# Attention row factors spread by a selection product instead of a round trip through DRAM, in a gated mix of attention and a gated feed-forward layer

## The chip, the cores and the metric

The kernel runs on one core of one Trainium2 chip. Time is device time in microseconds (us). Three runs of the kernel before gave a median of 1131.39 us (1130.17 to 1133.29). Engines are named as in the profile: PE (TensorE matmul), PEld (its weight loads), DVE (VectorE), ACT (ScalarE), POOL (GpSimd), SP (SyncE). A name with a q behind it (ACTq, SPq) is that engine's sequencer while it issues a DMA.

## The reference, cut to what matters

One input x of 2048 rows and 640 columns goes through a causal attention with a compressive memory (32 heads of width 20, four segments of 512 rows), through a gated feed-forward layer (hidden width 1728), and the two are mixed by a gate of each row.

```python
for s in range(N):                              # 4 segments of L = 512 rows
    logits = einsum("bhqd,bhkd->bhqk", qs, ks) * scale + mask
    p = softmax(logits)
    a_dot = einsum("bhqk,bhkd->bhqd", p, vs)
    num = einsum("bhld,bhde->bhle", phi(qs), M)
    den = einsum("bhld,bhd->bhl", phi(qs), z)[..., None] + 1e-6
    outs.append(g * num / den + (1.0 - g) * a_dot)   # g = sigmoid(beta), one per head
    M = M + einsum("bhld,bhle->bhde", phi(ks), vs)
    z = z + einsum("bhld->bhd", phi(ks))
a = stack(outs) @ wo
b = (silu(x @ w1) * (x @ w3)) @ w2
out = gate * a + (1 - gate) * b                 # gate = sigmoid((x * gate_w).sum(-1))
```

## The kernel before, in words

**Layout.** Everything is kept turned: features on partitions, the 512 rows of a segment c along the free axis. A matrix of 640 features is five blocks of 128 partitions. Single-precision products are done in three passes (high by high, high by low, low by high), so that one 128x512 output of a projection is a group of 15 matmuls in one PSUM bank. PSUM's eight banks are handed out in a ring (`bank_tile`, L110): a product that is spread over several steps holds its bank until it is filled, all others take the next in order, and a bank is taken again when its last reader is done.

**Order of the work.** The order on PE is the program's, written by hand. Attention runs as a fixed sequence of visits (`attention`, L744): for each group of four heads a long visit (score products `s`, transposed score products `t`, and the products `o` with the values) and a short one. Between visits a driver (the loop at L940) steps through a list of dense jobs (projections `q`, `k`, `v`, the feed-forward's `g`, `u` up and `f` down, the output projection `op`) in generators: each `yield` gives the time in ns that the step counts for. A yield that is a whole number also counts as a step for loading and splitting weights (`w_step`, L172), for late stores, and for `braid` (L839), which puts one step of a second generator behind every so many whole steps of a first. A yield that is a float (699.0) is no such step. `after(n, f)` (L727) runs f a number of slots later. The orders on DVE, ACT, POOL and SP are chosen by a scheduler at build time, except where `here(...)` pins an instruction to its program order. On each engine instructions run in order, and a DMA issue that waits holds up what is behind it.

**Around the change.** `pv_quad` (L626) writes each four heads' unscaled outputs and their row sums to DRAM (`od`). When the last heads of a segment are done, `o_sums` (L646) loads the sums as a 128x128 tile `rs` (32 heads by 4 pieces on partitions) and the gate's factors as `er`; 16 slots later `o_scale` (L667) takes the reciprocal on DVE (L669) and multiplies by (1-g) and the gate (L670). Then four DMAs issued by ACT (L672) write each head's factors 20 times to DRAM (`rd`, 32x20x512), and five more issued by ACT (`load_factor`, L682, issue at L686) read it back as five 128x512 tiles `rb`, through a ring of two buffers named `spread`, which the gate's own tile `sh` (`load_share`, L688) shares.

`normalize` (L703) is the first half of the output projection's job: for each of the five blocks DVE multiplies `oall` by `rb` (L711); from segment 1 on PE turns the memory's part with four transposes (`gt`, L715) and DVE adds it (L716); ACT rounds to the high part (L717) and DVE takes the low part (L718). It is braided into other work: for segment 0 and 2 into two up projections, one step behind every 3; for segment 1 into up projections, every 3 after 11; for segment 3, in the tail, into a down projection and up projections, every 3 after 10.

`ffn_down` (L516) fills one bank for each block of 128 outputs. With three hidden blocks that is 9 matmuls, with the last group (one whole and one half block) 5. The first 3 matmuls are a step that yields 699.0. For segment 0 the last down projection is braided with `split_x` (L237) of segments 2 and 3: ACT rounds x, copies it to a PSUM bank (`xh`) and DVE takes the difference (`X`, L131); what is left of segment 3's five blocks when the braid's first job ends is issued in a row.

Of the kernel before, what the change touches and what calls it, by code (L numbers as in the profile page):

```python
# [38 lines left out]
def gated_mix(ctx: ExitStack, tc: tile.TileContext, xT, wqk, wv, w13, w2, w2h, wo, beta, out):  # L39
# [9 lines left out]
    od = [dp.tile([H, 32, L], F32, name=f"od{c}") for c in range(NSEG)]  # L49
    gd = [dp.tile([P, 4, D], F32, name=f"gd{c}") for c in range(NSEG)]  # L50
    ed = [dp.tile([2, 4, P], F32, name=f"ed{c}") for c in range(NSEG)]
    rd = [dp.tile([H, DH, L], F32, name=f"rd{c}") for c in range(NSEG)]


    ident = cp.tile([P, P], F32, name="ident")
# [2 lines left out]
    vg = [cp.tile([P, 4, VG + 12], F32, name=f"vg{i}") for i in range(NVG)]  # L58
    gH = cp.tile([P, H], F32, name="gH")
    cR = cp.tile([P, 1], F32, name="cR")  # L60
    rs = cp.tile([P, P], F32, name="rs")
    er = cp.tile([P, P], F32, name="er")
    et = cp.tile([8, P], F32, name="et")
    nsT = [cp.tile([P, 32], FR, name=f"ns{i}") for i in range(2)]
    gate = cp.tile([P, NSEG, 2, 4], F32, name="gate")
    Ms = {}
# [13 lines left out]
    def gates():  # L80
        here(nc.sync.dma_start(gH, beta.rearrange("(o h) -> o h", o=1).broadcast_to([P, H])))
        for i in range(4):
            here(nc.sync.dma_start(cR[i::4], beta.rearrange("(h o) -> h o", o=1)))
        for g in (gH, cR):
            here(nc.scalar.activation(g, g, AF.Exp, scale=-1.0))
            here(nc.vector.tensor_scalar(g, g, 1.0, None, op0=ALU.add))

        nc.vector.reciprocal(cR, cR)
        nc.vector.tensor_scalar(cR, cR, -1.0, 1.0, op0=ALU.mult, op1=ALU.add)

    here = tc.keep_in_program_order
    last = {}
# [286 lines left out]

    def gate_turn(c):  # L380
        ps = bank_tile(f"ge{c}")
        nc.tensor.transpose(ps[:8, :P], gate[:, c].rearrange("p x a -> p (x a)"), ident)
        nc.scalar.copy(et, ps[:8, :P])
        store_later(ed[c].rearrange("x a p -> (x a) p"), et, ("e", c))
# [131 lines left out]
    def ffn_down(cs, js, idx, last=()):  # L516
        first = js[0] == 0
        w2s = [w_get(i, idx[0]) for i in idx]
        for c in cs:
            if c in last:  # L520
                load_share(c)
            if first:
                accs[c] = slot(f"acc{c}")[:, :KB * L].rearrange("p (b n) -> p b n", b=KB)
            for fb in range(KB):
                ps = bank_tile(f"f{c}_{js[0]}_{fb}", 1300 if len(js) > 2 else 690)
                ms = []
                for j, w in zip(js, w2s):
                    for a, b in (PASSES if j < NF else ((0, 0), (0, 1))):
                        ms.append((w[:, b, fb * P:(fb + 1) * P], hts[c, j][:, a, :]))
                for n, (w, h) in enumerate(ms):  # L530
                    nc.tensor.matmul(ps, w, h, start=n == 0, stop=n == len(ms) - 1)  # L531
                    if n % 3 == 2 and n < len(ms) - 1:
                        yield 699.0 if n == 2 else 699
                filled()
                dst = accs[c][:, fb]
                if first:
                    nc.scalar.copy(dst, ps)
                elif c not in last:
                    nc.vector.tensor_add(dst, ps, dst)
# [106 lines left out]
    def o_sums(c):  # L646
        assert ("e", c) in stored
        here(nc.sync.dma_start(rs, od[c][:, DH].rearrange("h (a n) -> h a n", n=P)))
        here(nc.sync.dma_start(er, ed[c][1:2].broadcast_to([H, 4, P])))
        after(16 if c < NSEG - 1 else 3, o_scale, c)  # L650
        if c == NSEG - 1:
            o_load(c, KB - 1)
        else:
            after(6, o_load, c, KB - 1)

    def o_load(c, b):

# [6 lines left out]
            else:  # L664
                here(nc.sync.dma_start(dst, od[c][h, e:e + n]))

    def o_scale(c):  # L667

        here(nc.vector.reciprocal(rs, rs))  # L669
        nc.vector.scalar_tensor_tensor(rs, rs, cR, er, op0=ALU.mult, op1=ALU.mult)  # L670
        for a in range(4):
            here(nc.scalar.dma_start(rd[c][:, :, a * P:(a + 1) * P], rs[a::4].unsqueeze(1).broadcast_to([H, DH, P])))  # L672
        turned.append(c)
        for b in range(2):
            after(8 + b, load_factor, c, b)

    shares, factors = {}, {}

    def spread(name):
        return sp.tile([P, L], F32, tag="spread", name=name, bufs=2)  # L680

    def load_factor(c, b):  # L682
        if b < KB and (c, b) not in factors:
            assert c in turned
            factors[c, b] = spread(f"rb{c}_{b}")
            here(nc.scalar.dma_start(factors[c, b], rd[c].rearrange("h e n -> (h e) n")[b * P:(b + 1) * P]))  # L686
# [15 lines left out]

    def normalize(c):  # L703

        load_factor(c, 0)
        load_factor(c, 1)
        if not c:
            gms[c] = big_tile(f"oT{c}", FR)[:, :KB * L].rearrange("p (b n) -> p b n", b=KB)
        for b in range(KB):
            o, hi = factors[c, b], gms[c][:, b]  # L710
            nc.vector.tensor_mul(o, oall[c][:, b].bitcast(F32), o)  # L711
            if c:
                pt = bank_tile(f"gt{c}_{b}")
                for qb in range(4):
                    nc.tensor.transpose(pt[:, qb * P:(qb + 1) * P], hi[:, qb * P:(qb + 1) * P].bitcast(F32), ident)  # L715
                nc.vector.tensor_add(o, o, pt)  # L716
# [10 lines left out]
    def after(n, f, *a):  # L727
        soon.append([n, f, a])
# [147 lines left out]
    d = job_down(A, 2)  # L876
    u = [job_up(A, j) for j in GROUPS[3][:2]]
    o1, o2 = jobs_oproj(0)
    seg = [d, braid(chain(u), o1, 3), o2] + [job_up(A, j) for j in GROUPS[3][2:]] + [job_down(A, 3)]
# [16 lines left out]
    segs.append((2 * H + LAG + 2, seg))  # L896
    up.append(job_up(B, 2))
    o1, o2 = jobs_oproj(1)
    seg = [braid(chain(up[1:]), o1, 3, 11), braid(o2, job_read(3), 3, 1), job_down(B, 0), braid(chain(jobs_up(B, 1)), (0, load_memory(2)), 5)]
# [4 lines left out]
    seg = [d, braid(chain(u), o1, 3), o2] + [job_up(B, j) for j in GROUPS[2][2:]]  # L904
# [120 lines left out]
```

## Time and profile before

| | before |
|---|---|
| median of 3 runs | 1131.39 us (1130.17 to 1133.29) |
| the profiled execution's own time | 1133.55 us |
| its span, first to last instruction | 1131.7 us |
| mean granted TensorE clock | 0.987 |
| PE busy | 1099.8 us (97%), 6265 matmuls |
| DVE / ACT / POOL busy | 588.0 / 460.3 / 491.1 us |

The profile is one execution. In a view in order of time a row gives the start, the length, the engine (or its sequencer, q), the line in the kernel, the operation, output<-input, and in brackets the idle time of that engine before the row and what ended it; rows merge instructions of one kind that follow one another. In a view by stretches each engine has its busy time (and its instructions in brackets), and PEclk is the clock that TensorE was granted, as a share of full speed.

### The profile page before, as it was taken

To read this page: it belongs to the slowest core of one execution; us is meant where nothing else is said; L and a number is where in the kernel's file an instruction comes from. 1 tells how busy PE (TensorE), PEld (TensorE's weight loads), DVE (VectorE), ACT (ScalarE), POOL (GpSimd) and SP (SyncE) were. 2 spreads that over 40 slices of the span, in tenths; PEclk is the share of its full clock that TensorE was granted. 3 is DMA by queue.
4 is the path that set the end of the run, shared out by engine and by line. 5 is a ranking of instruction groups with operands and counts; after the bars stand their busy time and mean duration, and the time that the engine had idled before them with its cause. 6 is when DMAs were issued, how large, how long until landed. Compare 5 with 4: busy or idle time off the path is not lost.

```text
span 1131.7 us, 17920 instructions
## 1 busy us (share of the span) xinstructions
PE 1099.8 (97%) x6265; PEld 855.7 (76%) x6265; DVE 588.0 (52%) x1692; ACT 460.3 (41%) x952; POOL 491.1 (43%) x598
## 2 busy tenths in 40 slices
PE   9999999999999999998999996999999999999998
PEld 6988877777777777786977774776776777777786
DVE  5032564455555545474253674884556675561465
ACT  6255334543243324255365632535534353333130
POOL 4053444455353336233253343554754464354142
PEclk9999999999999999998999997999999899999999
DMA  8265943343455425434385967555656343543423
GB/s 319 87 234 202 267 110 90 93 119 90 100 120 137 121 68 163 125 110 131 112 270 201 296 197 185 133 158 132 168 135 160 98 125 91 119 107 87 121 77 112
DMA packets 99193, 163.29 MB, mean 144 GB/s; under 512 B 10432, under 2 KB 34272, under 8 KB 99104
## 3 DMA queue, kind: packets, MB, share of 16 engines
q1 hardware_dynamic: 61312, 105.91, 29.9%
q0 software_dynamic: 20384, 38.68, 15.4%
q10 hardware_dynamic: 17408, 17.57, 4.9%
q8 instruction: 50, 0.82, 0.3%
q14 instruction: 39, 0.32, 0.1%
HBM read 101.80 MB, written 59.79 MB: 143 GB/s over the span
## 4 chain that ended last, share of the span: by engine, by line
PE 78%; issue 8%; DMA 5%; DVE 4%; POOL 3%; ACT 2%; ACTq 1%; SPq 0%; DVEq 0%; POOLq 0%
PE g L251 15%; PE f L531 15%; PE u L251 14%; PE q L251 6%; PE k L251 6%; PE o L631 5%; PE op L788 4%; PE s L578 4%; PE v L362 3%; PE t L611 3%; PE pm L425 1%; DVE junk L585 1%; POOL W L106 1%; PE nd L329 1%; DMA rb<-rd 1%
## 5 line engine op out<-in xcount | busy, mean ns | idle before, releaser
L106 POOL TENSOR_TENSOR W<-wr,W 128x640 fp32r<-128x640 f32 (+1 forms) x126 | 197.9, 1576 | 287.9 <-ACT W L105 263.1
L585 DVE CUSTOM_DVE_ANT_0 junk<-s,mask 128x256 bf16<-128x256 f32 (+3 forms) x512 | 250.4, 489 | 118.8 <-PE s L578 86.6
L617 ACT ACTIVATE P<-t 128x512 f32<-128x512 f32 (+1 forms) x384 | 172.0, 538 | 146.4 <-PE t L611 116.0
L251 PE MATMUL g<-X,W 128*128 128x512 f32 x840 | 209.8, 398 | 1.5 <-ACT P L617 1.4
L531 PE MATMUL f<-ht,W 128*128 128x512 f32 x820 | 198.4, 400 | 0.0
L251 PE MATMUL u<-X,W 128*128 128x512 f32 x780 | 196.5, 399 | 0.3 <-DVE m L585 0.3
L251 PEld LDWEIGHTS g<-X,W 128*128 128x128 f32 x840 | 155.6, 188 | 38.4 <-ACT P L617 1.6
L531 PEld LDWEIGHTS f<-ht,W 128*128 128x128 f32 x820 | 154.9, 191 | 37.3 <-issue 0.2
L621 POOL TENSOR_SCALAR_AFFINE_SELECT P<-P 128x256 f32<-128x256 f32 x192 | 94.0, 500 | 195.8 <-ACT P L617 195.2
L251 PEld LDWEIGHTS u<-X,W 128*128 128x128 f32 x780 | 143.8, 188 | 35.7 <-DVE m L585 1.2
L105 ACT CAST W<-wr 128x640 fp32r<-128x640 f32 (+1 forms) x133 | 95.7, 728 | 111.6 <-PE f L531 24.8
L106 POOL TENSOR_TENSOR ht<-ft,ht 128x512 fp32r<-128x512 f32 x52 | 68.0, 1307 | 97.3 <-ACT ht L105 97.3
L631 PE MATMUL o<-P,vg 128*32 128x512 f32 (+3 forms) x1024 | 79.8, 455 | 9.9 <-DVE rb L716 9.5
L555 POOL DMA_DIRECT2D qk<-qkd x128 | 82.8, 649 | 3.4 <-PE t L611 2.5
L578 PE MATMUL s<-qk 60*128 60x256 f32 (+3 forms) x512 | 77.4, 348 | 4.2 <-DVE oq L635 2.7
L251 PE MATMUL k<-X,W 128*128 128x512 f32 x300 | 77.0, 403 | 0.9 <-ACT P L617 0.9
L251 PE MATMUL q<-X,W 128*128 128x512 f32 x300 | 73.8, 400 | 1.4 <-ACT X L105 0.6
L631 PEld LDWEIGHTS o<-P,vg 128*32 128x32 f32 x1024 | 31.0, 113 | 54.6 <-issue 44.7
L362 PE MATMUL v<-W,X 128*128 128x320 f32 (+1 forms) x480 | 71.8, 311 | 0.0
L362 PEld LDWEIGHTS v<-W,X 128*128 128x128 f32 x480 | 71.1, 189 | 0.4
L611 PE MATMUL t<-qk 62*128 62x256 f32 (+3 forms) x512 | 65.0, 326 | 6.2 <-DVE X L131 3.6
L251 PEld LDWEIGHTS q<-X,W 128*128 128x128 f32 x300 | 55.6, 189 | 16.6 <-ACT W L105 1.2
(107 smaller groups left out, 1096.0 us busy)
## 6 DMA issues: line engine op xcount, KB each, us to landing
qk<-qkd POOLq DMA_DIRECT2D x128, 240.0 KB, 4.2
wr<-in_w_dram SPq DMA_DIRECT2D x80, 320.0 KB
qkd<-qs SPq DMA_DIRECT2D x20, 512.0 KB
qkd<-ks SPq DMA_DIRECT2D x20, 512.0 KB
od<-oq SPq DMA_DIRECT2D x32, 256.0 KB
wr<-in_wo_dram SPq DMA_DIRECT2D x20, 320.0 KB
vg<-vd SPq DMA_DIRECT2D x16, 336.0 KB
xr<-in_xT_dram SPq DMA_DIRECT2D x20, 256.0 KB
```

The lines of the kernel that those rows point to most:

```text
L105: pin(nc.scalar.copy(dst[:, 0], src))
L106: (lo or nc.gpsimd.tensor_sub)(dst[:, 1], src, dst[:, 0].bitcast(F32))
L251: nc.tensor.matmul(ps, w[:, a, kb * P:(kb + 1) * P], x[:, b, kb, :], start=n == 0, stop=n == 14)
L362: nc.tensor.matmul(ps[:, :n1 - n0], x[:, a, kb, lb * P:(lb + 1) * P], wvt[kb][:, b, n0:n1], start=n == 0, stop=n == 14)
L531: nc.tensor.matmul(ps, w, h, start=n == 0, stop=n == len(ms) - 1)
L555: here(nc.gpsimd.dma_start(t[64 * i:64 * i + RH], qkd[c][RH * (h + i):RH * (h + i + 1)]))
L578: nc.tensor.matmul(ps[i][:, o:o + w], q[:, qb * P:(qb + 1) * P], key[:, :w], start=n == 0, stop=n == len(todo) - 1, skip_group_check=True)
L585: nc.vector.tensor_tensor_reduce(out=junk[:, :w], in0=ps[i][:, o:o + w], in1=mask[:, L - w:], scale=1.0, scalar=-3.0e38, op0=ALU.add, op1= ...
L611: nc.tensor.matmul(ps[i][:, o:o + L - kb * P], key[:, kb * P:(kb + 1) * P], q[:, kb * P:], start=n == 0, stop=n == len(todo) - 1, skip_gro ...
L617: last["exp"] = nc.scalar.activation(pairs[2 * m + k]["P"][:, i, o:o + n], ps[i][:, b:b + n], AF.Exp, scale=SCALE)
L621: nc.gpsimd.affine_select(d, d, pattern=[[0, 2], [0, n], [1, P]], base=0, channel_multiplier=-1, compare_op=ALU.is_ge, fill=0.0)
L631: nc.tensor.matmul(ps[32 * i:32 * i + 32, kb * P:], heads[2 * p + i]["v"][:, kb], pairs[p + i // 2]["P"][:, i % 2, o:o + n], start=kb == 0 ...
```

## The change

1. `rd` in DRAM, its four writes and the five reads of `rb` go. In their place DVE splits the 128x128 factors into three bfloat16 parts (two copies and two differences), and three DMAs issued by SP, pinned in order, lay the parts out as one tile `rR` of 96 partitions by 512 (three times 32 heads).
2. A constant `sel` of 96x640 in bfloat16 is made once on POOL: three times the same 32x640 matrix of ones and zeros that is one where the column belongs to the row's head.
3. `normalize` takes a bank for each block, fills it with one matmul of `sel`'s 128 columns with `rR` (`rr`), and DVE multiplies `oall` by that bank into a tile of the ring `f`. One step of 700 for a block replaces two steps.
4. `o_scale` comes 22 slots after the sums instead of 16. The braids that carry `normalize` take a step behind every 5 (segments 0 and 2) or 4 (segments 1 and 3) instead of 3, and its time in the plan is 3.5 instead of 0 or 2.3.
5. The tile `spread` goes; `sh` has a buffer of its own or, for segment 3, one of the ring `f`. `er` and `et` move to a ring of two that the memory's update uses.
6. In `ffn_down` the first step of a fill of 5 matmuls yields 699 instead of 699.0, so that such a fill counts as two steps.

```diff
-    rd = [dp.tile([H, DH, L], F32, name=f"rd{c}") for c in range(NSEG)]
+    sel = cp.tile([96, D], BF, name="sel")
     rs = cp.tile([P, P], F32, name="rs")
-    er = cp.tile([P, P], F32, name="er")
-    et = cp.tile([8, P], F32, name="et")
+    rp = cp.tile([P, 3, P], BF, name="rp")
+    rR = cp.tile([96, L], BF, name="rR")
...
+    def selection():
+        here(nc.gpsimd.memset(sel, 1.0))
+        nc.gpsimd.affine_select(sel[:32], sel[:32], pattern=[[1, D]], base=0, channel_multiplier=-DH,
+                                compare_op=ALU.is_ge, fill=0.0)
+        nc.gpsimd.affine_select(sel[:32], sel[:32], pattern=[[-1, D]], base=DH - 1, channel_multiplier=DH,
+                                compare_op=ALU.is_ge, fill=0.0)
+        for i in (32, 64):
+            nc.gpsimd.tensor_copy(sel[i:i + 32], sel[:32])
...
     def gate_turn(c):
+        et = sp.tile([8, P], F32, tag="mt", name=f"et{c}", bufs=2)
...
                     if n % 3 == 2 and n < len(ms) - 1:
-                        yield 699.0 if n == 2 else 699
+                        yield 699.0 if n == 2 and len(ms) > 5 else 699
...
     def o_sums(c):
+        er = sp.tile([P, P], F32, tag="mt", name=f"er{c}", bufs=2)
         here(nc.sync.dma_start(er, ed[c][1:2].broadcast_to([H, 4, P])))
-        after(16 if c < NSEG - 1 else 3, o_scale, c)
+        after(22 if c < NSEG - 1 else 3, o_scale, c, er)
...
+    def o_scale(c, er):
+        here(nc.vector.reciprocal(rs, rs))
+        nc.vector.scalar_tensor_tensor(rs, rs, cR, er, op0=ALU.mult, op1=ALU.mult)
+        nc.vector.tensor_copy(rp[:, 0], rs)
+        nc.vector.tensor_sub(rs, rs, rp[:, 0])
+        nc.vector.tensor_copy(rp[:, 1], rs)
+        nc.vector.tensor_sub(rp[:, 2], rs, rp[:, 1])
+        for i in range(3):
+            here(nc.sync.dma_start(rR[32 * i:32 * i + 32].rearrange("h (a n) -> h a n", n=P), rp[:, i]))
+        turned.append(c)
...
-    def o_scale(c):
-        here(nc.vector.reciprocal(rs, rs))
-        nc.vector.scalar_tensor_tensor(rs, rs, cR, er, op0=ALU.mult, op1=ALU.mult)
-        for a in range(4):
-            here(nc.scalar.dma_start(rd[c][:, :, a * P:(a + 1) * P], rs[a::4].unsqueeze(1).broadcast_to([H, DH, P])))
-        turned.append(c)
-        for b in range(2):
-            after(8 + b, load_factor, c, b)
-    def load_factor(c, b):
-        if b < KB and (c, b) not in factors:
-            factors[c, b] = spread(f"rb{c}_{b}")
-            here(nc.scalar.dma_start(factors[c, b], rd[c].rearrange("h e n -> (h e) n")[b * P:(b + 1) * P]))
     def load_share(c):
-        shares[c] = spread(f"sh{c}")
+        shares[c] = f_tile("sh") if c == NSEG - 1 else sp.tile([P, L], F32, tag="share", name=f"sh{c}", bufs=1)
...
     def normalize(c):
-        load_factor(c, 0)
-        load_factor(c, 1)
         for b in range(KB):
-            o, hi = factors[c, b], gms[c][:, b]
-            nc.vector.tensor_mul(o, oall[c][:, b].bitcast(F32), o)
+            o, hi = f_tile(f"on{c}_{b}"), gms[c][:, b]
+            ps = bank_tile(f"rr{c}_{b}")
+            nc.tensor.matmul(ps, sel[:, b * P:(b + 1) * P], rR, start=True, stop=True)
+            nc.vector.tensor_mul(o, oall[c][:, b].bitcast(F32), ps)
...
             nc.vector.tensor_sub(oall[c][:, b], o, hi.bitcast(F32))
-            yield 450 if c else 1
-            load_factor(c, b + 2)
-            yield 1
+            yield 700
...
-        return (2.3 if c else 0, a), (17.5, b)
+        return (3.5, a), (17.5, b)
...
-    seg = [d, braid(chain(u), o1, 3), o2] + ...
+    seg = [d, braid(chain(u), o1, 5), o2] + ...
-    seg = [braid(chain(up[1:]), o1, 3, 11), ...
+    seg = [braid(chain(up[1:]), o1, 4, 11), ...
-    tail = [braid(chain([d] + u), o1, 3, 10)] + [o2, job_down(B, 4, B)]
+    tail = [braid(chain([d] + u), o1, 4, 10)] + [o2, job_down(B, 4, B)]
...
+        elif n == 4:
+            selection()
```

More of the change, by code (lines that the diff above doesn't have):

```diff
@@ L654, in o_sums @@
             after(6, o_load, c, KB - 1)
+    def o_scale(c, er):
[8 more added lines that the diff above has]
+        turned.append(c)
+    shares = {}
     def o_load(c, b):
@@ L665, in o_load @@
                 here(nc.sync.dma_start(dst, od[c][h, e:e + n]))
-    def o_scale(c):
-        here(nc.vector.reciprocal(rs, rs))
-        nc.vector.scalar_tensor_tensor(rs, rs, cR, er, op0=ALU.mult, op1=ALU.mult)
-        for a in range(4):
-            here(nc.scalar.dma_start(rd[c][:, :, a * P:(a + 1) * P], rs[a::4].unsqueeze(1).broadcast_to([H, DH, P])))
-        turned.append(c)
-        for b in range(2):
-            after(8 + b, load_factor, c, b)
-    shares, factors = {}, {}
-    def spread(name):
-        return sp.tile([P, L], F32, tag="spread", name=name, bufs=2)
-    def load_factor(c, b):
-        if b < KB and (c, b) not in factors:
-            assert c in turned
-            factors[c, b] = spread(f"rb{c}_{b}")
-            here(nc.scalar.dma_start(factors[c, b], rd[c].rearrange("h e n -> (h e) n")[b * P:(b + 1) * P]))
     def load_share(c):
-        shares[c] = spread(f"sh{c}")
+        shares[c] = f_tile("sh") if c == NSEG - 1 else sp.tile([P, L], F32, tag="share", name=f"sh{c}", bufs=1)
         here(nc.scalar.dma_start(shares[c], ed[c][0].rearrange("a n -> (a n)").unsqueeze(0).broadcast_to([P, L])))
@@ L703, in normalize @@
     def normalize(c):
-        load_factor(c, 0)
-        load_factor(c, 1)
+        assert c in turned
         if not c:
@@ L878, in gated_mix @@
     o1, o2 = jobs_oproj(0)
-    seg = [d, braid(chain(u), o1, 3), o2] + [job_up(A, j) for j in GROUPS[3][2:]] + [job_down(A, 3)]
+    seg = [d, braid(chain(u), o1, 5), o2] + [job_up(A, j) for j in GROUPS[3][2:]] + [job_down(A, 3)]
     u0, u1 = jobs_up_by_chunk(A, 4)
@@ L898, in gated_mix @@
     o1, o2 = jobs_oproj(1)
-    seg = [braid(chain(up[1:]), o1, 3, 11), braid(o2, job_read(3), 3, 1), job_down(B, 0), braid(chain(jobs_up(B, 1)), (0, load_memory(2)), 5)]
+    seg = [braid(chain(up[1:]), o1, 4, 11), braid(o2, job_read(3), 3, 1), job_down(B, 0), braid(chain(jobs_up(B, 1)), (0, load_memory(2)), 5)]
     segs.append((3 * H + LAG + 1, seg))
@@ L903, in gated_mix @@
     o1, o2 = jobs_oproj(2)
-    seg = [d, braid(chain(u), o1, 3), o2] + [job_up(B, j) for j in GROUPS[2][2:]]
+    seg = [d, braid(chain(u), o1, 5), o2] + [job_up(B, j) for j in GROUPS[2][2:]]
     seg += [job_down(B, 2), braid(chain(jobs_up(B, 3)), (0, load_memory(3)), 5)]
```

## The prediction

> **What bounds the kernel now.** I read the page's busy shares first, then what PE waited for, then PE's busy time in stretches of 20 us, and last the order of time in the stretches that fall short.
>
> ```profile
> span 1131.7 us, 17920 instructions
> PE 1099.8 (97%) x6265; PEld 855.7 (76%) x6265; DVE 588.0 (52%) x1692; ACT 460.3 (41%) x952; POOL 491.1 (43%) x598
> PE o L631 <- DVE rb L716: 9.5, 1, 9.5
> core 0: us, PE busy (x) PEld busy (x) DVE busy (x) ACT busy (x) POOL busy (x), PEclk, DMA share, GB/s
> 383.00:403.00 20.00, 19.49 (x95) 15.05 (x96) 14.41 (x36) 9.67 (x20) 9.78 (x13) 1.00 0.42 120
> 503.00:523.00 20.00, 16.02 (x78) 10.71 (x81) 12.77 (x23) 11.52 (x21) 7.81 (x13) 0.89 0.52 169
> 686.00:706.00 20.00, 10.18 (x63) 5.78 (x63) 6.55 (x12) 4.41 (x8) 3.61 (x4) 0.67 0.58 163
> 869.00:889.00 20.00, 17.26 (x101) 12.20 (x100) 10.20 (x31) 5.42 (x13) 4.21 (x8) 0.83 0.41 113
> 1053.00:1089.00 36.00, 36.00 (x168) 29.33 (x167) 20.58 (x29) 8.70 (x14) 7.92 (x5) 1.00 0.40 122
> ```
>
> PE sets the end: it is idle for 1131.7 - 1099.8 = 31.9 us, and everything else hides behind it. So an edit is worth what it takes from PE's idle time, from the time at a lower granted clock, or adds to PE's stream. Three stretches hold 3.98 + 9.82 + 2.74 = 16.5 us of the idle time, and they alone (the last with its neighbours) show a clock under 1. Segment 0's (383 to 403) loses 0.51 us, segment 3's (1053 to 1089) nothing. The worst of the three is segment 1's normalize:
>
> ```profile
> 684.20 5.85 ACTq L672 DMA_DIRECT2D rd<-rs x4
> 694.75 0.81 ACTq L686 DMA_DIRECT2D rb<-rd x2
> 698.55 1.37 DVE L711 TENSOR_TENSOR rb<-oall,rb 128x512 f32<-128x512 f32 x2 [5.96 <-DMA rb<-rd]
> 700.77 4.49 PE L631 MATMUL o<-P,vg 128*32 128x512 f32 x32 [9.46 <-DVE rb L716]
> 849.07 2.36 PE L631 MATMUL o<-P,vg 128*32 128x512 f32 x32
> 877.07 0.79 PE L578 MATMUL s<-qk 60*128 60x384 f32 x3 [2.74 <-DVE oq L635]
> 877.79 8.55 PE L531 MATMUL f<-ht,W 128*128 128x512 f32 x24
> 875.72 0.69 DVE L711 TENSOR_TENSOR rb<-oall,rb 128x512 f32<-128x512 f32 x1 [3.48 <-DMA rb<-rd]
> 1114.34 11.70 PE L531 MATMUL f<-ht,W 128*128 128x512 f32 x50
> ```
>
> ACT spends 5.85 us on issuing four writes, waits for their landing to issue the reads, DVE waits for the reads, and PE stands for 9.46 us because banks and exponentials are behind both. Then 32 `o` matmuls take 4.49 us where they normally take 2.36: half clock. Segment 2 has the same in small at 874: DVE waits at L711, its copy `oq` is late, PE idles 2.74 us, and 24 `f` matmuls take 8.55 us where 24 x 11.70 / 50 = 5.62 would do.
>
> The third, at 513, has nothing to do with `rb`:
>
> ```profile
> 507.42 3.63 PE L251 MATMUL q<-X,W 128*128 128x512 f32 x15
> 510.89 2.36 PE L362 MATMUL v<-W,X 128*128 128x320 f32 x15
> 515.07 0.50 PE L611 MATMUL t<-qk 62*128 62x512 f32 x1 [0.95 <-DVE X L131]
> 516.51 0.44 PE L611 MATMUL t<-qk 62*128 62x384 f32 x1 [0.94 <-DVE X L131]
> 518.66 0.79 PE L611 MATMUL t<-qk 62*128 62x384 f32 x3 [1.71 <-DVE X L131]
> 519.82 4.49 PE L631 MATMUL o<-P,vg 128*32 128x512 f32 x32 [0.37 <-DVE X L131]
> ```
>
> Here four blocks of segment 3's x are split in a row, each through a bank, and the visit waits for those banks: 3.98 us idle, then `o` at half clock again.
>
> **The change, part by part.** Removed waits first.
>
> (a) Segment 1. Idle 20 - 10.18 = 9.82 us. After 700.77 the clock stays at half until about 706 (0.33 x 20 x 2 = 13.2 us of half clock in the stretch, most of it while idle): 5.2 us of work at half speed, 2.6 lost. Sum 12.4.
> (b) Segment 2. 2.74 idle, and 8.55 - 5.62 = 2.9 with 0.4 for the three `s` at half clock. Sum 6.0.
> (c) The split of x. 3.98 idle, 4.49 - 2.36 = 2.1 on `o` and about 1.1 on the fills around it: 7.2.
>
> (a) and (b) hang on the round trip through DRAM, which goes: no ACT instruction waits for a landing, no DVE instruction for `rb`. I take both in full. Segment 0's 0.51 I leave out.
>
> New on PE: twenty `rr` matmuls of 128x512. The tightest row for that shape is the fill above, 11.70 / 50 = 0.234 us each, 4.7 us in all, all of it in PE's stream. Upper bound: the weight load isn't hidden, 0.19 us more each:
>
> ```profile
> L531 PEld LDWEIGHTS f<-ht,W 128*128 128x128 f32 x820 | 154.9, 191 | 37.3 <-issue 0.2
> ```
>
> That gives 8.5; the lower bound is 4.7, since PE streams 512 columns either way. I take 4.7, because that row's loads (and `gt`'s) lie under the matmul before.
>
> New wait: the first `rr` of a segment needs `rR`. In the changed order of segment 1 that is tightest: `u`, which DVE's L670 stands behind, then `g`, then a long visit, then `rr`.
>
> ```profile
> 678.74 3.65 PE L251 MATMUL g<-X,W 128*128 128x512 f32 x15
> 848.16 0.50 PE L578 MATMUL s<-qk 60*128 60x512 f32 x2
> 852.67 3.79 PE L251 MATMUL u<-X,W 128*128 128x512 f32 x15
> 679.74 0.68 DVE L497 SCALAR_TENSOR_TENSOR ft<-fu,u 128x512 f32<-128x512 f32 x1
> 1053.85 0.59 SPq L648 DMA_DIRECT2D rs<-od  x1
> 1056.16 0.95 DVE L669 RECIPROCAL rs<-rs 128x128 f32<-128x128 f32 x1 [0.26 <-DMA rs<-od]
> 1057.15 0.35 DVE L670 SCALAR_TENSOR_TENSOR rs<-rs,cR,er 128x128 f32<-128x128 f32 x1
> 1066.80 0.60 PE L715 MATMUL gt<-ident,gm 128*128 128x128 f32 x4
> 56.59 3.09 POOL L106 TENSOR_TENSOR W<-wr,W 128x640 fp32r<-128x640 f32 x2 [30.29 <-ACT W L105]
> ```
>
> PE takes 3.5 us for `g` and 852.67 - 848.16 = 4.5 for the visit: 8.0 after the end of `u`. `rR` takes 0.7 (L497), 0.35 (L670), four 128x128 operations at no more than 0.35 each, one more SP issue of 0.59 and a landing of 1056.16 - 1053.85 = 2.3: 5.3. It is hidden with 2.7 us to spare. In segments 0 and 2 a down projection of 90 matmuls (21 us) lies between; in the tail `gt` stands at 1066.80 now and `rR` would land near 1062. On SP the three issues stand in front of weight loads for the output projection, which are used 15 us and more later; ahead of them stands one weight load whose buffer POOL has emptied by then. On DVE the four new operations (at most 1.4 us a segment) are covered by its 48% idle time; ACT loses 36 DMA issues. `sel`'s five operations fall into POOL's idle 30.29 us ahead of 56.59.
>
> New waits that I do expect: in segment 1 ACT's cast of a weight tile waits for the end of the second `u`, and DVE's rounding chain and the row maxima queue behind it; the next visit may wait for their DMA. Nearest row: the `rb` wait's cousin of 0.94 us above, from 0 to 2.74; I take 1.5.
>
> (d) The short fills. As two steps each, ten fills give ten more whole steps to the braid (every 4), so three of segment 3's four blocks move in among the fills. What is late next? DVE. It has the down projection's sums and the gate there already:
>
> ```profile
> 501.36 1.29 DVE L513 TENSOR_TENSOR acc<-acc,sh 128x512 f32<-128x512 f32 x2 [0.95 <-DMA sh<-ed]
> 507.97 1.88 DVE L539 TENSOR_TENSOR acc<-f,acc 128x512 f32<-128x512 f32 x3
> 512.87 0.69 DVE L285 SCALAR_TENSOR_TENSOR pq<-q,phi_t 128x512 f32<-128x512 f32 x1
> 513.72 0.69 DVE L585 CUSTOM_DVE_ANT_0 junk<-s,mask 128x512 bf16<-128x512 f32 x1 [0.16 <-PE s L578]
> ```
>
> From 501.36 it has 19 operations of about 0.6 us (a pitch of 1.88 / 3) in the new order: until 512.8. Behind them come one maximum (0.65), the low part of q, another maximum and `pq`: 515.3. The new order puts the visit straight behind `q` (ends at 511.0), before `v`, and with a block's bank between, `o` takes the bank that `q` had, which `pq` releases. PE gets there at about 512.8 and waits until 515.3: 2.5 us idle in place of 3.98. Bounds: 0 and 3.98. Whether the clock halves after it is open: the smallest gap that did it here was 2.74 us (segment 2). 2.5 is nearest to 2.74, so I take 3.2 us, as in (c): 5.7 left of 7.2.
>
> Sum: -12.4 - 6.0 - (7.2 - 5.7) + 4.7 + 1.5 = -13.7 us. The profiled execution took 1133.55 us, span 1131.7 and 1.85 around it, 2.2 above the median of 1131.39. Applied to the median: 1117.7.
>
> The Trainium skill ("TensorE: Matmul & The Clock Gate", What's actually happening) says that the clock halves after an idle window of about 3.4 us. Segment 2's row of 2.74 us shows half clock after less, so here the measurement decides; by the page the 2.5 us gap would keep full clock, and the sum would be the first rival's.
>
> **The rivals.**
> - The gap at 513 stays, the clock doesn't halve: 3.2 less, 1114.5. For it: no gap under 2.7 shows half clock. Against: 2.5 is close, and windows fall where they fall. The rule just named is this rival.
> - No gap at 513 at all and no new wait in segment 1: 1117.7 - 5.7 - 1.5 = 1110.5. Against it: DVE's count above.
> - New bank waits of the old kind: `rr` takes a bank more per block, and DVE, in order, waits for PE where it waited for DMA. If segment 2 keeps a gap like its own (6.0) and segment 1 doubles the 1.5: 1125.2. For it: DVE is still the engine that frees those banks; against: nothing there waits 3.48 us any more.
> - Slower: `rR` is late, and PE, which never waited for `rb` directly, now stands at `rr` in its own stream. The place is SP's queue:
>
> ```profile
> 1056.53 21.65 SPq L162 DMA_DIRECT2D wr<-in_wo_dram  x3
> 680.43 13.54 SPq L162 DMA_DIRECT2D wr<-in_wo_dram  x3
> ```
>
> Such loads hold SP until POOL frees a buffer. With `rR` behind one, segment 1 loses 13.54 - 2.7 = 10.8 and 2.6 of clock, the tail 21.65 - 5 = 16.6 and 2.6: 32.6, so 1150. It decides from 13.7 us of lateness in sum. Against it: in the changed order the long-held loads stand behind `rR`.
> - `rr` at its upper bound, 8.5, moves any of these by 3.8.
>
> **How the numbers follow.** Forecast 0.44, clock stays 0.20, no gap 0.10, new bank waits 0.13, no change 0.04 (several of these waits together), slower 0.09. A measurement can tell about 0.3%, 3.4 us, from no change. Faster 0.87, same 0.04, slower 0.09. The range from 1108 to 1127 leaves out the slower case, no change and the ends: with `rr` at 8.5 the bank waits give 1129, with no gap and segment 0's 0.5 too it is 1110, and a fresh median can lie 2 us from this one, as the three runs do.
>
> **What would show it.** Right: no PE wait over 1 us between 680 and 710 and between 865 and 885 (both shift earlier), clock 1.00 there; twenty `rr` at a pitch near 0.234; a gap at `o` near 512 released by DVE's L285, 2 to 3 us; ACT without L672. Wrong: PE waiting for DMA `rR`, `rr` groups well over 0.3 us, half clock in a new place, or a gap at 512 as long as before.

## The result, and the profile after

The kernel after takes 1114.61 us (median of 4 runs, 1112.98 to 1115.99), the kernel before 1130.78 us on the same chip in the same rounds: ratio 0.9853, 95% interval 0.9832 to 0.9874, or 16.2 us. The profiled execution of after took 1114.77 us, close to its median; that of before, 1133.55 us, lay 2.8 us above its own. So the two traces differ by 18.7 us of span, and the working below is held against those.

The page of the kernel after, its first lines:

```profile
span 1113.0 us, 17965 instructions
PE 1096.1 (98%) x6285; PEld 853.2 (77%) x6285; DVE 587.6 (53%) x1708; ACT 461.9 (41%) x952; POOL 494.9 (44%) x603
```

PE is idle for 16.9 us instead of 31.9, and busy for 3.7 us less although it has 20 matmuls more: less of its time runs at half clock. Where it went is seen when both spans are cut at the same instructions: the `q` fill ahead of the split of x, the first `g` of segment 1's braid, and the first `op` of segments 1, 2 and 3. Stretches of the kernel before (the first two numbers are the ends, then the length and PE's busy time):

```profile
0.00:507.42 507.42, 503.14 (x2766) 396.88 (x2767) 245.98 (x698) 209.07 (x428) 216.47 (x267) 1.00 0.50 142
507.42:678.74 171.32, 165.84 (x1031) 133.98 (x1030) 84.58 (x257) 85.87 (x186) 67.25 (x94) 0.98 0.63 201
678.74:733.47 54.73, 44.83 (x269) 31.94 (x268) 34.11 (x100) 21.27 (x44) 25.50 (x34) 0.88 0.63 159
733.47:931.58 198.11, 192.91 (x1189) 143.84 (x1188) 124.20 (x404) 85.02 (x179) 102.22 (x124) 0.98 0.54 139
931.58:1096.84 165.26, 163.87 (x892) 125.75 (x890) 83.39 (x216) 56.89 (x114) 66.95 (x74) 1.00 0.38 104
```

The same stretches of the kernel after:

```profile
0.00:507.38 507.38, 504.10 (x2771) 397.48 (x2772) 245.24 (x701) 213.14 (x434) 220.93 (x272) 1.00 0.48 137
507.38:671.83 164.45, 162.47 (x1032) 132.77 (x1031) 84.74 (x257) 82.39 (x180) 67.81 (x94) 1.00 0.65 208
671.83:720.34 48.51, 45.25 (x274) 31.92 (x273) 36.37 (x107) 21.71 (x45) 25.36 (x33) 0.96 0.54 128
720.34:911.54 191.20, 190.02 (x1193) 141.85 (x1191) 121.72 (x406) 85.19 (x178) 100.87 (x125) 1.00 0.50 132
911.54:1078.20 166.66, 165.08 (x896) 125.86 (x895) 84.03 (x220) 57.37 (x114) 69.11 (x75) 1.00 0.33 88
```

| stretch | measured | by the prediction's terms |
|---|---|---|
| start and segment 0 | 0.0 | +1.2 (five `rr`) |
| split of x | -6.9 | -1.5 |
| segment 1 | -6.2 | -9.7 (-12.4, five `rr`, new wait 1.5) |
| segment 2 | -6.9 | -4.8 (-6.0, five `rr`) |
| tail | +1.4 | +1.2 (five `rr`) |
| rest | -0.1 | 0 |
| sum | -18.7 | -13.7 |

Two stretches miss by much, on opposite sides. The split of x in the kernel after, PE's weight loads with their waits, and DVE:

```profile
512.21 0.67 DVE L142 TENSOR_TENSOR X<-xr,xh 128x512 fp32r<-128x512 f32 x1
...
512.94 0.16 PEld L643 LDWEIGHTS o<-P,vg 128*32 128x32 f32 x8 [0.30 <-DVE X L142]
...
514.63 0.68 DVE L296 SCALAR_TENSOR_TENSOR pq<-q,phi_t 128x512 f32<-128x512 f32 x1
...
515.36 0.19 PEld L623 LDWEIGHTS t<-qk 62*128 62x128 f32 x2 [0.33 <-DVE pq L296]
```

`pq` ends at 515.31, as forecast (515.3). But `o` starts at 512.94, right after the `X` of one block: it takes that block's bank, and the `t` behind `o` takes the bank that `q` had. By the time `t` is there, `o` has covered the wait. Nothing of the gap is left but tenths, and the clock stays full.

Segment 1 in the kernel after, PE in order of time:

```profile
682.36 0.50 PE L590 MATMUL s<-qk 60*128 60x512 f32 x2
685.07 0.73 PE L623 MATMUL t<-qk 62*128 62x512 f32 x6 [2.21 <-DMA qk<-mr]
685.73 3.98 PE L643 MATMUL o<-P,vg 128*32 128x512 f32 x32
...
690.94 0.39 PE L717 MATMUL rr<-rR,sel 96*128 96x512 bf16 x1
```

The gap of 9.46 us at `o` is gone and `rr` does not wait for `rR`, but a new gap of 2.21 us stands at `t`, which waits for the row maxima's DMA, and `o` behind it runs at half clock (3.98 us instead of 2.36). The DMA issues around it in order of time, and then, from the view of the tile `qk`, the times from issue to landing of its DMAs over the whole run:

```profile
670.10 1.80 POOL L705 DMA_DIRECT2D gm<-gd  x2
...
673.53 4.20 SPq L173 DMA_DIRECT2D wr<-in_wo_dram  x2
...
675.59 1.08 ACTq L611 DMA_DIRECT2D qk<-mr  x2
```

```profile
DMA to landing us min/median/max: 3.2/4.3/9.8
```

With the median's 4.3 us it would have landed near 680.5, before `t` was due. It took about 9: by the trace's records of the semaphore that a DMA raises as it lands, the second of the two, issued at 676.14, landed at 684.93.

### The profile page after: what moved, and what is told of

It reads as the page before. It is cut to its first block, busy times and chain, and to the rows that moved or that the text cites. A ratio compares the mean times of both kernels' runs of the same rounds, so it can differ in the third digit from the quotient of the medians.

```text
span 1113.0 us, 17965 instructions
## 1 busy us (share of the span) xinstructions
PE 1096.1 (98%) x6285; PEld 853.2 (77%) x6285; DVE 587.6 (53%) x1708; ACT 461.9 (41%) x952; POOL 494.9 (44%) x603
## 4 chain that ended last, share of the span: by engine, by line
PE 87%; issue 3%; DMA 3%; DVE 3%; ACT 2%; POOL 2%; SPq 0%; ACTq 0%; DVEq 0%; POOLq 0%
PE g L262 16%; PE f L543 16%; PE u L262 15%; PE v L373 6%; PE k L262 6%; PE q L262 6%; PE o L643 6%; PE s L590 4%; PE op L793 4%; PE t L623 3%; PE pm L437 1%; PE nd L340 1%; DMA qk<-mr 1%; ACT P L629 1%; POOL W L117 1%
## 5 line engine op out<-in xcount | busy, mean ns | idle before, releaser
L643 PE MATMUL o<-P,vg 128*32 128x512 f32 (+3 forms) x1024 | 77.2, 443 | 0.2
L503 DVE SCALAR_TENSOR_TENSOR fu<-ft,g 128x512 f32<-128x512 f32 x52 | 35.7, 686 | 70.1 <-ACT ft L502 69.8
L551 DVE TENSOR_TENSOR acc<-f,acc 128x512 f32<-128x512 f32 x65 | 44.7, 689 | 44.8 <-PE f L543 44.6
```

The costliest lines, as they stand in the source:

```text
L643: nc.tensor.matmul(ps[32 * i:32 * i + 32, kb * P:], heads[2 * p + i]["v"][:, kb], pairs[p + i // 2]["P"][:, i % 2, o:o + n], start=kb == 0 ...
```

## The experiments

Each was timed against the kernel before on the same chip; a ratio is to that. "After" is 0.9853 (0.9832 to 0.9874). The runs are spread over several chips, so a difference to after is safer by the ratios than by the medians; under some 3 us neither is clear of noise, and there the stretches of the traces decide.

**The two parts by themselves.** The short fills alone, in the kernel before:

```diff
-                        yield 699.0 if n == 2 else 699
+                        yield 699.0 if n == 2 and len(ms) > 5 else 699
```

> The kernel before with the line of the short fills alone (they count as two steps), the way through DRAM unchanged. Theory A, from the trace after: the whole gap at the split of x goes (3.98 us idle and 3.2 at half clock, 0.4 us left over), so 6.5 to 7.2 us faster than before, about 1124.2. Theory B, the sum of the prediction: 2.5 us of the gap and the half clock stay, so 1.5 us faster, about 1129.3. Segment 1's wait of 9.5 us and segment 2's of 2.7 us stay in both.

And the opposite, the kernel after with that line as it was:

> The kernel after with the short fills counted as one step, as before. Theory A: it loses the 6.5 to 7.2 us of the split of x and keeps the rest, about 1121.5; the three waits for X near 515 us are there again with about 4 us idle and half clock behind them. Theory B: it loses 1.5 us only, about 1116.

Measured: 1123.87 us, ratio 0.993 (0.9909 to 0.9951), for the fills alone: theory A. But 1115.19 us, 0.9844 (0.9802 to 0.9886), without them: near the time of theory B, but not by its mechanism, since the gap that theory B keeps is not there. Each part removes the gap at the split without the other. PE with the fills alone, in order of time and as the stretch from `q` to segment 1's `g`; then PE with the sums alone:

```profile
515.65 2.36 PE L631 MATMUL o<-P,vg 128*32 128x512 f32 x32 [0.71 <-DVE X L131]
```

```profile
507.71:671.87 164.16, 162.13 (x1031) 132.86 (x1030) 84.75 (x256) 82.50 (x180) 67.80 (x94) 1.00 0.65 210
```

```profile
510.69 0.63 PE L623 MATMUL t<-qk 62*128 62x512 f32 x6
511.25 2.36 PE L643 MATMUL o<-P,vg 128*32 128x512 f32 x32
...
516.21 3.96 PE L373 MATMUL v<-W,X 128*128 128x320 f32 x25 [1.18 <-ACT P L629]
```

With the fills alone the visit stays behind the first `v`, but only two blocks of x come between `q` and it, instead of five (the prediction read four from the waits). With the sums alone one block does, since the visit moves ahead of `v`: the sums' part changes the number of steps and their times in the plan, and so the place of visits far from its own lines. So the 7.6 us of the fills are not additional to the sums' part: the stretch from `q` to that `g` takes 171.32 us in the kernel before, 164.16 with the fills alone, 164.29 with the sums alone and 164.45 with both. What the fills bring in the kernel after these runs cannot tell from nothing.

**What cost in the trip through DRAM: the trip, or ACT's queue?** The kernel before with another issuer:

```diff
-            here(nc.scalar.dma_start(rd[c][:, :, a * P:(a + 1) * P], ...
+            here(nc.sync.dma_start(rd[c][:, :, a * P:(a + 1) * P], ...
-            here(nc.scalar.dma_start(factors[c, b], rd[c]...
+            here(nc.sync.dma_start(factors[c, b], rd[c]...
```

> The kernel before with the writes to rd and the reads of rb issued on SP's queue in place of ACT's; the trip through DRAM itself stays. Theory A: the trip is what costs. DVE still waits about 6 us for rb in segment 1 and 3 in segment 2, at best the 5.85 us of issues is taken off ACT: 0 to 4 us faster, 1127 to 1131, or slower if SP's stores of o queue behind the trip. Theory B: ACT's queue is what costs, with its exponentials behind 5.85 us of issues and a landing: most of 18.4 us comes back, 1116 to 1120.

Measured: 1130.95 us, ratio 0.999 (0.9965 to 1.0015): theory A, and at its lower end. Segment 1 of that kernel in order of time:

```profile
683.47 6.69 SPq L672 DMA_DIRECT2D rd<-rs  x4
...
697.58 1.40 DVE L711 TENSOR_TENSOR rb<-oall,rb 128x512 f32<-128x512 f32 x2 [5.36 <-DMA rb<-rd]
...
699.83 4.29 PE L631 MATMUL o<-P,vg 128*32 128x512 f32 x32 [7.85 <-DVE rb L716]
```

ACT is free of the issues and PE still waits 7.85 us. From the first write to the first product of `rb` are 14 us on either queue (684.20 to 698.55 in the kernel before, 683.47 to 697.58 here). In segment 2 the queue had a share: with SP, DVE waits 1.99 us for `rb` instead of 3.48, PE 0.47 and 0.72 us instead of 2.74, and the 24 `f` take 7.39 us instead of 8.55. The median shows next to nothing of it. So what pays is that the trip is gone; only in segment 2 does part of it hang on ACT's queue.

**The price of `rr`.** Each of the twenty issued four times:

```diff
-            nc.tensor.matmul(ps, sel[:, b * P:(b + 1) * P], rR, start=True, stop=True)
+            for _ in range(4):
+                nc.tensor.matmul(ps, sel[:, b * P:(b + 1) * P], rR, start=True, stop=True)
```

> The kernel after with each of the 20 rr matmuls issued four times into the same bank (each starts the sum afresh, so the last one counts): 60 more matmuls. Theory A: all of it lies in PE's stream at 0.23 us each, 14.0 us slower than after, about 1128.6. Theory B: their own weight load isn't hidden, 0.39 us each, 23 us slower, about 1138. Theory C: PE has slack there and part is hidden, under 10 us slower.

Measured: 1124.76 us, 0.9937 (0.9918 to 0.9956), 10.2 us above after by the medians and 9.5 by the ratios. In the tail, where nothing else moves:

```profile
1053.89 1.04 PE L718 MATMUL rr<-rR,sel 96*128 96x512 bf16 x4
1054.77 0.60 PE L723 MATMUL gt<-ident,gm 128*128 128x128 f32 x4
```

From the first `rr` to `gt` 0.88 us, against 0.23 for one: 0.22 for each more, 13.0 for sixty, all in PE's stream. Part of the difference to 10.2 went where PE would have waited: in the traces its busy time grows by 11.6 us and its idle time falls from 16.9 to 1122.4 - 1107.7 = 14.7, so that the span grows by 9.4. So the price of one product is theory A's, the sum lies at theory C's bound, as some of it is absorbed, and theory B's 0.39 is out.

**How much slack has `rR`?** The parts taken through three DRAM copies first:

```diff
+        here(nc.sync.dma_start(rh[c][0], rp))
+        for i in range(2):
+            here(nc.sync.dma_start(rh[c][i + 1], rh[c][i]))
         for i in range(3):
-            here(nc.sync.dma_start(rR[...], rp[:, i]))
+            here(nc.sync.dma_start(rR[...], rh[c][2][:, i]...))
```

> The kernel after with the three parts of the factors taken through three DRAM copies in a row on SP before they are loaded into rR: each needs a landing of the one before, about 2.9 us (0.6 issue, 2.3 landing), so rR comes 8.7 us later in every segment. Theory A, from the slack in the trace after (rR issued by 683.0, landed near 685.3, needed at 690.9 in segment 1; issued by 1040.5, landed near 1042.7, needed at 1047.7 in the tail): PE waits about 3 us at the first rr of segment 1 and 4 us at the tail's, up to 3 us of half clock behind each, nothing in segments 0 and 2: 7 to 13 us slower than after, 1122 to 1128. Theory B: the weight loads queued behind the copies on SP are what hurts: waits at op in the output projections, over 15 us slower. Theory C: there is more slack than that: under 3 us.

Measured: 1127.79 us, 0.9951 (0.9926 to 0.9975), 13.2 us above after by the medians and 11.1 by the ratios: the upper part of theory A. Its first `rr` of segment 1 and of the tail:

```profile
696.85 0.61 PE L722 MATMUL rr<-rR,sel 96*128 96x512 bf16 x1 [3.32 <-DMA rR<-rh]
...
1058.92 0.38 PE L722 MATMUL rr<-rR,sel 96*128 96x512 bf16 x1 [2.29 <-DMA rR<-rh]
```

That is 5.6 us of waits. Of the 11.5 us between the two spans, 4.6 lie in segment 1 and 4.1 in the tail, but not all of them come from `rR`: some 1.6 of the tail's are a spell of half clock near 945, away from any `rr`. Another 2.9 us lie in the first 510 us, where PE waits for no `rr`; that execution has a spell of half clock at 9.64. So `rR` explains some 7 us, the bottom of theory A, and the rest was not foreseen. PE waits nowhere for the weights of `op`, so theory B is out. The slower rival had the right mechanism: where `rR` is late, PE stands, and in segment 1 the clock then stayed at half for 6.8 us.

The times and braids of before, with the products kept:

```diff
-        after(22 if c < NSEG - 1 else 3, o_scale, c, er)
+        after(16 if c < NSEG - 1 else 3, o_scale, c, er)
-        return (3.5, a), (17.5, b)
+        return (2.3 if c else 0, a), (17.5, b)
-    seg = [d, braid(chain(u), o1, 5), o2] ...        (segments 0 and 2)
+    seg = [d, braid(chain(u), o1, 3), o2] ...
-    seg = [braid(chain(up[1:]), o1, 4, 11), ...      (segment 1; the tail alike, with 10)
+    seg = [braid(chain(up[1:]), o1, 3, 11), ...
```

> The kernel after with the braids, the scaling's due time and the prices of before (a step of normalize after every third fill, 16 slots, 2.3 or 0): products with the selection matrix stay. In segment 1 the first rr then stands in front of a visit, behind 12 of g's 15 matmuls, and not behind it. Theory A: rR, which landed near 685 in the kernel after, is late there: PE waits 2 to 5 us at rr, with half clock behind it, and the wait at t is covered by that; 0 to 5 us slower than after, 1115 to 1120. Theory B: the due time of 16 brings rR forward by as much: no wait at rr, same as after or 2 us faster.

Measured: 1117.98 us, 0.9874 (0.9851 to 0.9898), 3.4 us above after by the medians and 2.4 by the ratios, whose intervals overlap. The trace shows theory A's wait at `rr`, and then segments 1 and 2 as stretches, cut as above:

```profile
684.83 0.38 PE L717 MATMUL rr<-rR,sel 96*128 96x512 bf16 x1 [4.24 <-DMA rR<-rp]
```

```profile
670.69:720.41 49.72, 44.89 (x275) 32.06 (x273) 37.96 (x107) 21.67 (x45) 25.21 (x33) 0.97 0.54 125
720.41:914.01 193.60, 190.40 (x1193) 141.94 (x1191) 121.91 (x406) 84.65 (x178) 100.47 (x124) 1.00 0.51 131
```

`rR` was issued by 679.95 here, and `rr` started 4.9 us later. But this wait takes the place of the one at `t`, and segment 1 is only 1.2 us longer than in the kernel after (49.72 and 48.51); segment 2 is longer by 2.4 (193.60 and 191.20), with two waits of 1.03 and 0.91 us for DVE's maxima. So the later place of `rr` in segment 1 is worth about 1 us in these traces, and the products with the old times still save 14 (1132.1 for the kernel before in those rounds).

**What makes the row maxima late in segment 1?** First the loads of `gm` begun later, by six and by twelve steps:

```diff
-    seg += [braid(braid(up[0], r, 2), (0, load_memory(1)), 3, 10)]
+    seg += [braid(braid(up[0], r, 2), (0, load_memory(1)), 3, 16)]   (or 22)
```

> The kernel after with the loads of segment 1's memory product (gm from gd) begun six steps later in their braid: two of the four go to POOL's queue behind the next casts. It asks what makes the row maxima's DMA in segment 1 land 9.4 us after its issue where 4.3 is the median, and PE wait 2.21 us at t. Theory A: the traffic of the gm loads just ahead of it. Then the landing falls towards 5 to 7 us, the wait at t under 1 us and the half clock behind it go, 3 to 4.5 us faster than after, about 1110.5. Theory B: the weight and q/k loads are what fills the engines, or ACT's late issue is the cause: no change within 1 us, about 1114.6. Theory C: the two later loads stand in the maxima's way instead, or gt waits for gm: 1 to 6 us slower.

> The same with the loads begun twelve steps later: all four behind the q/k loads, three of them behind the next hidden block's cast. Theory A: the maxima's DMA lands in about 4.3 us and the wait at t goes, but gm may be late for gt near 691: between 1110 and 1116. Theory B: the wait at t stays at 2 us, about 1114.6 or more.

Measured: 1111.1 us, 0.981 (0.9789 to 0.9832), and 1110.29 us, 0.9806 (0.9783 to 0.9828): theory A in both (by the ratios 4.9 and 5.3 us below after). With twelve steps, segment 1 in order of time, and then as a stretch of 20 us:

```profile
674.78 1.08 ACTq L611 DMA_DIRECT2D qk<-mr  x2
675.75 2.62 POOL L705 DMA_DIRECT2D gm<-gd  x3
...
681.90 0.63 PE L623 MATMUL t<-qk 62*128 62x512 f32 x6
```

```profile
680.00:700.00 20.00, 19.00 (x128) 13.11 (x128) 17.66 (x52) 10.34 (x22) 11.12 (x14) 1.00 0.48 120
```

No wait at `t`, full clock, and the fastest kernel of this study, 4.3 us below after by the medians; in the traces 4.1 us of it lie in segment 1. But this edit moved two things: with POOL's queue free the weight loads (L173) also start 4.0 us earlier, at 669.51 instead of 673.53 (0.8 of it because the whole execution is ahead). Three runs were meant to tell them apart. The first issues `gm` at its old place, but by SP:

```diff
-            here(nc.gpsimd.dma_start(gms[c]...
+            here((nc.sync if c == 1 else nc.gpsimd).dma_start(gms[c]...
```

> The kernel after with the four gm loads of segment 1 at their old place in the order, but issued on SP's queue in place of POOL's. The two kernels that began the loads later moved two things at once: the gm traffic, and (as POOL was free earlier for its part of a weight's split) the two weight loads on SP, from 673.5 to 670.5 us. Theory A: the gm traffic ahead of the maxima's DMA is what delays it. It is still ahead, so PE's wait at t stays at 1.5 to 2.5 us with half clock behind it: 1113 to 1116. Theory B: POOL's 5 us of issues delay its subtraction and so the weight loads into the maxima's way. With POOL free the weight loads start near 670.5, the wait at t goes: 1109 to 1111.5. Theory C: gm is now so late or SP so busy that rs and rR come late and PE waits at rr: over 1116.

Measured: 1113.42 us, 0.9851 (0.9825 to 0.9876), by the time theory A. But in its trace PE waited 0.57 us at `t` and not 2.21, with no half clock behind it, although the weight loads were almost as late as in after (1.2 us behind the start of `g`, against 1.7). Segment 1 as a stretch:

```profile
674.54:719.81 45.27, 43.69 (x274) 31.46 (x273) 36.30 (x107) 21.59 (x45) 22.41 (x29) 1.00 0.48 122
```

That is 3.2 us less than in after. The span is only 0.9 us shorter because the first 510 us of that execution took 2.7 us more, with half clock from 7.81 to 14.64. So the time says little here, and the wait fits neither theory. The second holds POOL with six tiny copies in place of the loads:

```diff
+                        here(nc.gpsimd.dma_start(idle[k + ...], ed[0]))
```

> The kernel with the gm loads twelve steps later, and in the place where they were issued before, six tiny copies from DRAM to DRAM (4 KB each, used by nothing) that hold POOL for about as long (6 of some 0.6 us against 4 of 0.9) and move next to nothing. The chain of the weights is then as late as in the kernel after (POOL's subtraction near 672, the weight loads near 673.5), and the gm traffic is still behind the maxima's DMA. Theory A: it is the gm traffic ahead of the maxima that makes them late. No wait at t, about 1110.3 as without the copies. Theory B: it is the weight loads, 3 us later because of POOL, that the maxima meet. PE waits 1 to 2.5 us at t with half clock behind it: 1113 to 1116.

Measured: 1111.34 us, 0.9829 (0.9806 to 0.9851), no wait at `t`. It tells nothing: the copies had no buffer to wait for, went out at 662.9 and 665.8, and the weight loads started at 669.93 as if they were not there. The third puts seven small loads into `gm` itself there, which wait for the same buffer:

```diff
+                if i == 15:
+                    for k in range(7):
+                        r = slice(16 * k, 16 * k + 16)
+                        here(nc.gpsimd.dma_start(gms[1].bitcast(F32)[r, 0, :P], gd[1][r, 0, :P]))
```

> The six copies of the run before held POOL too early, as they waited for no buffer; the gm loads wait on POOL until PE's last nd has read the buffer that gm takes (3.6 us, to 666.9). Here seven small loads (8 KB each) into gm itself stand in the old place, so POOL waits the same and then issues for some 3.5 us; the four whole loads follow behind the maxima's DMA, as in the kernel with the loads twelve steps later. Theory A: the gm traffic ahead of the maxima is the cause. POOL's subtraction and the weight loads are late (near 673.5), but PE does not wait at t (under 0.6 us): about 1110.5. Theory B: the late weight loads are. PE waits 1 to 2.5 us at t with half clock behind it: 1113 to 1116.

Measured: 1112.93 us, 0.9851 (0.9825 to 0.9876). In order of time:

```profile
666.35 3.46 POOL L910 DMA_DIRECT2D gm<-gd  x7 [3.60 <-PE nd L340]
...
672.78 4.15 SPq L173 DMA_DIRECT2D wr<-in_wo_dram  x2
...
682.11 0.63 PE L623 MATMUL t<-qk 62*128 62x512 f32 x6
...
687.34 0.38 PE L718 MATMUL rr<-rR,sel 96*128 96x512 bf16 x1 [0.99 <-ACT P L629]
```

POOL and the weight loads are as late as in the kernel after (1.5 us behind the start of `g`), and PE does not wait at `t`. So late weight loads alone don't make that wait, and theory A is left: the `gm` traffic ahead of the maxima. The semaphore records of five traces bear it out. They give the time from issue to landing of the second of the maxima's two DMAs in segment 1:

| kernel | `gm` loads issued ahead of it | landing, us | PE's wait at `t`, us |
|---|---|---|---|
| after | four | 8.8 | 2.21 |
| by SP | four | 7.2 | 0.57 |
| six steps later | three | 6.5 | none |
| twelve steps later | one | 4.2 | none |
| seven small loads, the four behind | 56 KB in all | 3.6 | none |

Why four cost less when SP issues them is left open. The Trainium skill ("DMA: Bandwidth & Descriptors", Queues, rings and completion order) says that a DMA's semaphore is written only after every earlier write of the same DMA engine, across queues. That agrees: with three of the four loads issued 1 us behind the maxima they landed in time, with three or four ahead of them late. No run here tells it from mere sharing of the engines. The time with the small loads is 1.7 us below after by the medians and level with it by the ratios, as here PE waits 0.99, 0.96 and 0.67 us at the first two `rr` and a `gt`, and has 3.4 us of half clock after them; why those came is left open.

## Why the prediction was right, and where it was not

- **(a), (b), the trip through DRAM: right.** The wait at `o` and the one in segment 2 are gone whole. Segment 2, PE after:

```profile
860.08 5.83 PE L543 MATMUL f<-ht,W 128*128 128x512 f32 x24
...
873.12 0.39 PE L717 MATMUL rr<-rR,sel 96*128 96x512 bf16 x1
873.35 0.60 PE L722 MATMUL gt<-ident,gm 128*128 128x128 f32 x4
```

  Its 24 `f` take 5.83 us instead of 8.55. The stretch gained 2.1 us more than forecast. Its idle time fell by 5.20 - 1.18 = 4.0 and not 2.74, since smaller waits ahead of that gap and behind it went or shrank too; the other 0.8 us, of PE's busy time, stays unexplained.
- **`rr` at 0.234: right.** The pitch is 873.35 - 873.12 = 0.23, and four in a row confirm it. In the first stretch those 1.2 us do not show, because almost as much idle time went there (4.28 to 3.28), of which the prediction had left out 0.51.
- **`rR` hidden: right.** No wait in any segment. It was closer than the 2.7 us to spare: in segment 1 `rR` landed at 685.52 by its semaphore, 6.6 us after the end of `u` and not 5.3, so 1.4 us were left of the 8.0.
- **(d), the gap at 513 with 5.7 us left: wrong, the largest error (5.4 us).** The step that failed is "`o` takes the bank that `q` had": the count of banks was off by one. `q` holds its bank until it is filled; the block, split during that fill, took a bank that stands in the ring ahead of `q`'s, and so `o` gets the block's bank. DVE was as late as forecast; what waited for it stood one group further back, covered by `o`. The rival "no gap" had this right. The rival "the clock doesn't halve" gives 1114.5, almost the measured time, but its mechanism, a gap of 2.5 us at full clock, did not come: that agreement is luck. The premise of that rival and of the forecast's 3.2 us for the clock, that the smallest gap with half clock behind it is 2.74 us, was wrong on the prediction's own rows: at 513 no single gap was longer than 1.71 us, and `o` ran at half clock (the last section says why). The step also put the visit's new place down to the short fills; the runs show that the sums' part moves it.
- **The new wait in segment 1, 1.5 us: the right place, too small, and for the wrong reason.** PE did wait for the maxima's DMA, for 2.21 us and within the bounds of 0 to 2.74; with two waits of about 0.5 behind it the stretch has 54.73 - 44.83 = 9.9 us of idle time before and 3.3 after, and 1.7 us went to half clock, which the term did not have. Together 5.0 instead of 1.5. The chain through ACT's cast and DVE's rounding was not what made it: issued as early as in the kernel with the loads twelve steps later, which does not wait, the DMA landed late behind the `gm` loads, which the prediction did not look at. Of the prediction's signs of being wrong, one came with it: half clock in a new place, from 686.31 to 689.72.
- That the sum came near is partly luck: the two errors cancel in part (-5.4 and +3.5), the rest is -3.1, in the start with segment 0 and in segment 2, so the sum was 5.0 us short in the traces. Against the medians it was 3.1 us off (1114.61 for 1117.7, inside the range), as the profiled execution of before lay above its median and that of after did not.

## What to carry to other kernels

Broadcasting small factors by a matmul with a matrix of ones and zeros cost 0.23 us for 128x512 and here replaced a write and a read-back that took 14 us from first issue to first use, whether ACT or SP issued them; the saving is as large as the wait it ends, and the factors must arrive before PE reaches the product, since PE now waits itself. Two edits that each move an order can remove the same gap: test them apart before adding their gains. A tiny DMA on the critical path should be issued ahead of large ones that are not yet needed; here 12 steps' delay of such loads was worth 4 to 5 us.

## What was not expected of the hardware

In these traces the clock goes by a grid of 3.41 us, and not by the length of a gap. When the stretches are cut at the start of a spell of half clock, every spell in a trace lies on whole multiples of 3.41 us: those of the kernel before begin at 518.52, 692.60 and 876.92, 51.0 and 54.0 windows apart. The kernel after, then the kernel before (length, PE busy, ... granted clock third from last; the first row of before is the window with two of the gaps at 513):

```profile
682.90:686.31 3.41, 1.24 (x14) 0.82 (x18) 1.91 (x5) 1.63 (x4) 1.55 (x1) 1.00 0.22 61
686.31:689.72 3.41, 3.41 (x34) 1.17 (x23) 0.00 (x0) 1.33 (x3) 0.84 (x2) 0.50 0.36 101
```

```profile
515.11:518.52 3.41, 0.90 (x2) 0.33 (x2) 1.81 (x4) 3.38 (x8) 1.67 (x3) 1.00 0.52 205
...
764.28:767.69 3.41, 2.18 (x32) 1.17 (x20) 2.04 (x5) 1.66 (x4) 1.14 (x2) 1.00 0.51 177
...
873.50:876.91 3.41, 0.82 (x9) 0.49 (x5) 1.19 (x2) 2.19 (x6) 1.37 (x3) 1.00 0.48 154
876.91:880.32 3.41, 3.25 (x9) 2.55 (x10) 2.58 (x8) 0.00 (x0) 1.22 (x2) 0.50 0.77 202
```

Over the thirteen traces of this study, from 60 us on and without the last window of each, a window at full clock with PE busy for 1.54 us or less was followed by half clock 16 times of 16; with 2.24 us or more never; between these both occur. So a gap of 2.21 us cost 1.7 us more here, while the 2.29 us in the tail of the kernel with late `rR` cost nothing more, as two windows shared it (2.51 and 2.02 us busy). The grid lies differently in each execution, which may be one reason why the same kernel varies by a few us (argued, not tried). The Trainium skill ("TensorE: Matmul & The Clock Gate", What's actually happening) has such a window, free-running, of 3.4 us; there the clock falls after an idle one, and here one that was a third busy was enough.
